# A layernorm, state-space convolution and gated unit on one core: the first spectra loads on GpSimd's queue, kept sums loaded behind SyncE's own stores, strict turns one chunk earlier, a pause cut in two

## The chip, the cores and the metric

The kernel runs on one core of a Trainium2 chip. The metric is the device time of one execution in microseconds (us); three runs of the kernel before gave a median of 709.12 us (707.67 to 710.72). One more execution was taken by the hardware profiler: 711.45 us, of which 709.7 us lie between the first and the last instruction (the span). All rows shown below come from that execution.

## What is computed

x is 2048 tokens by 448 channels. It is normalised per token, and the result goes through two independent branches whose sums are added to x. Branch A is a convolution with a kernel K of 2048 taps per channel, made from 256 complex exponentials per channel; the reference does it by Fourier transforms. Branch B is a gated unit with 1792 hidden features.

```python
P = jnp.exp((A * dt[:, None])[:, :, None] * pos[None, None, :])
K = 2.0 * jnp.einsum("dn,dnl->dl", C, P).real
y = irfft(rfft(u_t, 2 * L) * rfft(K, 2 * L))[:, :, :L]        # + u * D_skip
...
h = _sigmoid(xn @ w_gate) * (xn @ w_up)                       # 448 -> 1792
return x + _A_ref(xn, ...) + h @ w_down                       # 1792 -> 448
```

## The kernel before

Two generators record the work: `conv()` (branch A) and `glu()` (branch B). The loop at the end of the kernel decides which of them records its next piece: the one whose share `done[i] / total[i]` of its own planned cost is smaller. Each `yield` gives the planned cost of the piece just recorded (`WK` for a third of a chunk, `WS` for a spectra step, and so on). When the list `turns` is not empty, the loop alternates strictly between the two instead. A scheduler then arranges the recorded instructions of each engine at build time; `tc.issue_after(x)` asks that what follows stands behind `x`.

**Stages.** Until about 110 us the input is normalised and the tables for K are made. From 150 to 525 us, K is made in 56 chunks (`NCK`) of 8 channels, in `kgen`: TensorE spreads phases into PSUM (`tr`, L533), ScalarE takes sines of them (`S`, L541 to L544), VectorE multiplies them by magnitudes into `Et` and `Ft` (L602 to L604; there is one `Ft` buffer), and 64 small matmuls (`ko`, L618) contract them. Every fourth chunk is followed by `dm` (L628), a copy `ks` (L631) and 32 small matmuls, the first Fourier stage (`kp`, `kq`, L559), whose result goes to the DRAM buffer `sk_d`. GLU work stands between these: the gate and up projections (`gu`, L710, three matmuls for each product, since each operand is held as a high and a low part), then ScalarE's `th`, VectorE's `gu` product (L721), ScalarE's `hh` (L726), VectorE's `hl` (L728), and the down projections (`po`, L816, "downs" below), which VectorE adds to `acc` (L821). Half 0 of the tokens is done before half 1; between them, at about 265 to 350 us, the tokens of half 1 are normalised, turned and put through their own first stage (L207 to L290, L694). This is called the crossing below.

From 525 us on `spectra` runs 17 steps. A step loads `sx`, `skl` and for a new row `tb` (function `loads`, L864), does the forward stage `there` (64 matmuls `pk`, `px`, L901, from PSUM to `kk` and `xx` by VectorE, L907 and L908), the product (two VectorE multiplications L914 and L915, two GpSimd sums L917 and L918), `halves` (L922, L923), and one step later the inverse `back` (L936), whose result `vt` goes through DRAM (`v_d`). The pieces of `glu()` that are left stand between the steps. Steps are numbered from 0; three steps' loads (`NLD`) are recorded ahead. `bk` is the constant table of `back` and lies in the memory that `wk`, the table of the first Fourier stage, held; `wf` is the table of the last stage. `ac` (L1025) are sums of half 0 that were parked in DRAM and are loaded again; the program records these loads in steps 7 to 10, and the profile has them issued at 538.85 us (three) and 541.94 us, in the first steps. From 680 us the last inverse results go through DRAM once more and the output is stored.

The matmuls of one step are bound to the last GLU matmul recorded before them (`sp_mm`, `glu_mm`), so TensorE's order in the spectra is the order in which the two generators take turns.

Of the kernel before, what the change touches and what calls it, by code (L numbers as in the profile page):

```python
# [28 lines left out]
NFT = F // 128  # L29
WK = 4.3  # L30
WS = 5
HOLE = 6
AHEAD = 34
WP = 5
WX = 2
HELD = 9
LASTS = 2
HP = 300
Y0 = (8, 1)
CP = D // 4  # L40
H = D // 2
# [8 lines left out]
NLD = 3  # L50
NTB = 4
NCK = D // DC
# [74 lines left out]
def s4d_glu_kernel(ctx, tc, io):  # L127
    nc = tc.nc
# [11 lines left out]
    x1_d = dram.tile([2, 2, 32, 64, H], F32, name="x1_d")  # L140
    sk_d = dram.tile([2, 8, 128, 7, 128], F32, name="sk_d")
# [311 lines left out]
    def kgen(pk):  # L453
# [128 lines left out]
        for g in range(NCK // NCH):  # L582
            for c in range(NCH):
                cn = g * NCH + c
                S = nxt
                me, mf = (m[:, 2 * DC * (c % 2) : 2 * DC * (c % 2) + 2 * DC] for m in mags)
                of = (cn + 9) // NCH
                if NCH * of < NCK and cn and c != 6:
                    if c == 7 or cn == 1:
                        more = powers(pms, of, fts, sins[0])  # L590
                    next(more)
                    if cn < 3:
                        next(more)
                if cn + 1 < NCK:
                    nxt = ahead(cn + 1)
                    if c % 2 == 1:
                        squares(coming[0])
                yield WK / 3
                Et = tl[f"Et{cn % 2}"]
                Ft = tl["Ft"]  # L600
                two = lambda ap: ap.unsqueeze(1).to_broadcast([128, 2, 2 * DC, 32])
                v.tensor_tensor(Et[:, :, :, 32:64], two(me[:, :, 32:64]), S[:, 1::-1], ALU.mult)  # L602
                v.tensor_tensor(Et[:, :, :, 0:32], two(me[:, :, 0:32]), S[:, 1:3, :, ::-1], ALU.mult)  # L603
                fts[:] = [v.tensor_tensor(Ft, two(mf), S[:, 3:5], ALU.mult)]  # L604
                if cn + 2 < NCK and c % 2 == 0:
                    coming = magnitudes(cn // 2 + 1)
                if c % 2 == 1:
                    mags = coming
                yield WK / 3
                if cn % 4 == 0:  # L610
                    ko = psc[-1].tile([128, 8, 64], F32, name="ko", bufs=1)
                with tc.issue_after(glu_mm[0].ins):
                    for q in range(2):
                        sl = 2 * (cn % 4) + q
                        for k in range(4):
                            h, cc = k // 2, k % 2
                            for j in range(4):
                                nc.tensor.matmul(  # L618
                                    ko[32 * j : 32 * j + 32, sl],
                                    Ft[:, cc, DC * h + 4 * q + j],  # L620
                                    Et[:, cc, DC * h + 4 * q + j],
                                    start=(k == 0),
                                    stop=(k == 3),
                                    skip_group_check=True,
                                )
                if cn % 4 == 3:
                    ks = tl["ks"]
                    nc.tensor.matmul(  # L628
                        ko[:, :, 0], ident, dm[:, cn // 4], start=False, stop=True, skip_group_check=True
                    )  # L630
                    nc.scalar.copy(ks.rearrange("p s (q b) -> p s q b", q=2), ko.rearrange("p s (b q) -> p s q b", q=2))  # L631
                yield WK / 3
                if cn % 4 == 2 and cn > 3 or cn + 1 == NCK:

                    with hp(HP) if cn + 1 == NCK else tc.issue_after(glu_mm[0].ins):
                        first_stage((cn - 3) // 4 if cn + 1 < NCK else cn // 4)
# [94 lines left out]
    def glu():  # L731
        stores, later = [], []
        for half in range(2):
# [3 lines left out]
            for fs_ in ORDER[half]:  # L737
# [14 lines left out]
                for n_, (f, t) in enumerate(order):  # L752
# [39 lines left out]
                        wts.append((dh, dl))  # L792
                    if half == 1 and fs_ is ORDER[1][0] and n_ in (1, 3):
                        q = 2 + n_ // 2
                        with tc.issue_after(marks[1].ins):
                            x_load(accs[q], 4 * q, 4, [nc.scalar])
                    yield 2.5
                    for s_ in end[n_] if cross else ():
# [41 lines left out]
    def spectra(pf):  # L840
# [19 lines left out]
        def work(n, sh, bufs):  # L860
            return spare[n].pop() if spare.get(n) else pf.tile(sh, F32, name=n, bufs=bufs)

        def loads(h, k):
            sx = pf.tile([128, 4, H], F32, name="sx", bufs=NLD)  # L864
            sk = pf.tile([128, 7, 4, 32], F32, name="skl", bufs=NLD)
            if k == 32:
                to = sx[:, 0:2]
                nc.sync.dma_start(to, x1_d[:, :, :, ::32].rearrange("h q b c d -> (q b c) h d"))
                for i in range(2):
                    nc.sync.dma_start(sk[:, :, i], sk_d[i, 0, :, :, :32])  # L870
                return None, sk, sx
            rows = x1_d[h].rearrange("q b (c k) d -> (q b c) (k d)", c=2)
            nc.sync.dma_start(sx.rearrange("p k d -> p (k d)"), rows[:, H * k : H * k + 4 * H])
            if k not in tabs:
                tabs[k] = pf.tile([128, 4, 64], F32, name="tb", bufs=NTB)
                nc.sync.dma_start(tabs[k], io["c_tab"][k // 4])
            tb = tabs.pop(k) if h else tabs[k]

            nc.sync.dma_start(sk.rearrange("p g k d -> p g (k d)"), sk_d[h, k // 4])
            return tb, sk, sx  # L880

        def after():
            return tc.issue_after(sp_mm[0].ins)
# [42 lines left out]
        def back(h, k, sd, engs=(nc.sync, nc.sync)):  # L926
            vts.append(vts.pop(0))
            vt = vts[-1]
            n = 2 if k == 32 else 4
            bt = t32[:, 1:].rearrange("p (q e) m -> p q e m", q=2) if k == 32 else bk  # L930
            with after():
                for e in range(2):
                    for g in range(n):
                        s = slice(32 * g, 32 * g + 32)
                        for p in range(2):
                            mm = nc.tensor.matmul(  # L936
                                pb[g // 2][64 * p : 64 * p + 64, g % 2, :H], bt[s, p, e], sd[s, p, e],
                                start=(e == 0), stop=(e == 1), skip_group_check=True,
                            )
            sp_mm[:] = [mm]  # L940
            for j in range(n // 2):
                nc.scalar.copy(vt[:, 2 * j : 2 * j + 2], pb[j][:, :, :H])  # L942

            for p in range(2):
                s = slice(64 * p, 64 * p + 64)
                real = slice(64 * p, 64 * p + 64, 2)
                to = lambda h_: v_d[h_, s].rearrange("(c g q) w d -> w c g q d", c=2, g=4)
                if k == 32:
                    for j in range(2):
                        engs[p].dma_start(to(j)[:, 1, 0, 0], vt[real, j])  # L950
                elif k == 0:
                    engs[p].dma_start(to(h)[:, 0, 0, 0], vt[real, 0])
                    for c in range(2):
                        engs[p].dma_start(to(h)[:, c, 1:, 0], vt[64 * p + c : 64 * p + 64 : 2, 1:])
                else:
                    engs[p].dma_start(to(h)[:, :, :, k // 4], vt[s])  # L956

        def turned(h, k, n=8, eng=nc.sync):
            if h not in vp:
# [33 lines left out]
        steps = [(0, k) for k in ks] + [(1, k) for k in ks[-NTB:] + ks[:-NTB]]  # L993
        steps[3:3] = [(None, 32)]
        tabs = {}
        ld = [loads(*s) for s in steps[:NLD]]
        nc.gpsimd.dma_start(wf, io["c_wf"])
        prev, made, wait, due = None, None, [], []
        turns[:] = [0]
        for n, (h, k) in enumerate(steps):  # L1000

            end = n + 1 == len(steps)
# [11 lines left out]
                ld.append(loads(*steps[n + NLD]))  # L1014
            glu_on[:] = [1]
            yield WS / 2
            sp_mm[:] = glu_mm
            if ready is not None:
                back(*ready)
                if ready[1] < 32:  # L1020
                    wait.append(ready[:2])
            if 7 <= n < 11:
                o = slice(2 * n - 14, 2 * n - 12)
                with after():
                    nc.sync.dma_start(ac[:, o], acc_d[:, o])  # L1025

            while len(wait) > 2 and not (due and wait[0][0] == 1):
# [25 lines left out]
    def conv():  # L1053
        with tc.tile_pool(name="psk", bufs=1, space=PSUM) as ps_, tc.tile_pool(
# [78 lines left out]
                            yield from x_spec([xns[n - 2][:, b + i] for i in range(2)], 4 * (n - 2) + b)  # L1133
            with tc.tile_pool(name="pk", bufs=1, side="right", reuse_waits="tile") as pk:
                yield from kgen(pk)
        yield HOLE
        psc.append(ctx.enter_context(tc.tile_pool(name="psf", bufs=1, space=PSUM)))

        pa = ctx.enter_context(tc.tile_pool(name="pa", bufs=1, side="left", reuse_waits="tile"))
# [2 lines left out]
            yield from spectra(pf)  # L1142

    lasts, glu_mm, sp_mm, glu_on, x1s, hfs, xls = [], [], [], [], [0], [], []
    turns = []
    xq, psc, raws, acl, marks, slots, pqs = list(x_first), [], [], [], [None, None], {}, []
    W1s, GGs, act = [], [], []
    gens = [conv(), glu()]
    total = [sum(Y0) + 11 * WP + 8 * WX + AHEAD + NCK * WK + HOLE + 19 * WS, 2 * (4 + NFT * 14.8) - HELD]
    done = [0.0, 0.0]  # L1150
    done[0] += next(gens[0])
    held = False
# [41 lines left out]
```

## Time and profile before

| | |
|---|---|
| median of 3 runs | 709.12 us (707.67 to 710.72) |
| profiled execution | 711.45 us, span 709.7 us |
| TensorE busy | 658.4 us, 93% of the span, 8581 matmuls |
| VectorE, ScalarE, GpSimd busy | 577.1, 418.6 and 381.1 us (81%, 59%, 54%) |
| mean granted TensorE clock | 0.969 |
| DMA | 125.76 MB, mean 177 GB/s |

A row of a timeline gives the start in us, the duration in us, the engine (PE is TensorE, DVE is VectorE, ACT is ScalarE, POOL is GpSimd, SP is SyncE; a "q" behind the name marks the issuing of a DMA), the line of the kernel, the instruction with the tile that it writes and those that it reads, the count, and in brackets how long the engine was idle before it and what ended that. A row of the windows gives the stretch in us, its length, the busy time and count of each engine, the granted TensorE clock as a fraction, the busy share of the DMA engines and their GB/s.

### The profile page before, as it was taken

How to read it: one execution, taken by the hardware profiler on the slowest of the kernel's cores; microseconds unless marked ns; L12 is line 12 of the kernel's file. 1: busy time of each engine (PE TensorE's matmuls, PEld its weight loads, DVE VectorE, ACT ScalarE, POOL GpSimd, SP SyncE). 2: the span in 40 equal slices, each digit the busy share in tenths (PEclk: the TensorE clock that was granted, in tenths of full speed). 3: DMA queues.
4: the chain of work that ended last, by engine and by line, in shares of the span. 5: the costliest groups of instructions: out<-in, count | busy, mean ns of one | idle time of the engine just before them, and what ended most of it. 6: DMA issues, size and time to landing. Idle time of an engine off the chain costs nothing. (4 is left out here: it accounts for less than half of the span.)

```text
span 709.7 us, 20759 instructions
## 1 busy us (share of the span) xinstructions
PE 658.4 (93%) x8581; PEld 506.8 (71%) x8581; DVE 577.1 (81%) x779; ACT 418.6 (59%) x651; POOL 381.1 (54%) x395
## 2 busy tenths in 40 slices
PE   2998999999998899898899999999996999999994
PEld 1765778888876687564678788788884777777783
DVE  5789899589989898986568798799868888986753
ACT  3635636479888958787457877987842333332220
POOL 2111016586799999965246769889913344342101
PEclk9998999999999999797899999999999999999998
DMA  9987658655225633465575314333369878887366
GB/s 197 254 272 217 189 180 247 225 194 197 44 90 154 198 92 90 107 166 135 161 214 165 101 54 140 108 100 94 95 196 292 294 286 278 291 279 223 131 180 159
DMA packets 96638, 125.76 MB, mean 177 GB/s; under 512 B 12976, under 2 KB 82928, under 8 KB 96288
## 3 DMA queue, kind: packets, MB, share of 16 engines
q1 hardware_dynamic: 78688, 111.52, 51.0%
q10 hardware_dynamic: 17136, 11.01, 6.6%
q0 software_dynamic: 720, 1.90, 1.2%
q8 instruction: 68, 1.11, 0.7%
q14 instruction: 26, 0.21, 0.1%
HBM read 72.09 MB, written 52.30 MB: 175 GB/s over the span
## 5 line engine op out<-in xcount | busy, mean ns | idle before, releaser
L511 POOL TENSOR_TENSOR me<-me,pm 128x32 f32<-128x32 f32 (+1 forms) x168 | 157.2, 935 | 71.8 <-DVE Et L603 58.8
L511 POOL TENSOR_TENSOR mf<-mf,pm 128x64 f32<-128x64 f32 (+1 forms) x112 | 115.8, 1034 | 6.5
L710 PE MATMUL gu<-xh,wh 128*128 128x512 f32 x336 | 101.9, 411 | 2.4 <-DVE hl L728 1.0
L710 PE MATMUL gu<-xl,wh 128*128 128x512 f32 x336 | 96.7, 393 | 0.0
L710 PE MATMUL gu<-xh,wl 128*128 128x512 f32 x336 | 96.3, 392 | 0.0
L816 PE MATMUL po<-dh,hh 128*128 128x448 f32 (+1 forms) x227 | 88.5, 390 | 3.6 <-ACT x L694 1.8
L602 DVE TENSOR_TENSOR Et<-me,S 128x1024 f32<-128x1024 f32 x56 | 75.9, 1357 | 14.6 <-ACT S L544 8.2
L816 PE MATMUL po<-dh,hl 128*128 128x448 f32 (+1 forms) x227 | 86.0, 379 | 0.7 <-DVE hl L728 0.7
L603 DVE TENSOR_TENSOR Et<-me,S 128x1024 f32<-128x1024 f32 x56 | 77.4, 1382 | 10.9 <-ACT me L524 10.0
L816 PE MATMUL po<-dl,hh 128*128 128x448 f32 (+1 forms) x227 | 85.7, 377 | 0.0
L604 DVE TENSOR_TENSOR Ft<-mf,S 128x1024 f32<-128x1024 f32 x56 | 80.8, 1442 | 5.8 <-ACT S L544 3.3
L917 POOL TENSOR_TENSOR yy<-yy 128x448 f32<-128x448 f32 (+1 forms) x16 | 31.0, 1940 | 91.1 <-DVE yy L914 91.1
L710 PEld LDWEIGHTS gu<-xh,wh 128*128 128x128 f32 x336 | 60.8, 191 | 25.6 <-issue 9.0
L726 ACT CAST hh<-gu 128x512 fp32r<-128x512 f32 x56 | 33.2, 594 | 72.1 <-DVE gu L721 65.0
L541 ACT ACTIVATE S<-tr 128x1024 f32<-128x1024 f32 x56 | 58.2, 1039 | 25.8 <-PE tr L533 14.2
L710 PEld LDWEIGHTS gu<-xh,wl 128*128 128x128 f32 x336 | 62.9, 188 | 14.5 <-DVE fr L305 0.7
L618 PEld LDWEIGHTS ko<-Et,Ft 128*32 128x32 f32 x3584 | 55.3, 113 | 24.7 <-issue 9.8
L710 PEld LDWEIGHTS gu<-xl,wh 128*128 128x128 f32 x336 | 62.7, 188 | 14.1 <-issue 0.7
L618 PE MATMUL ko<-Et,Ft 128*32 128x64 f32 x3584 | 65.4, 225 | 6.0 <-DVE Ft L604 5.6
L821 DVE SCALAR_TENSOR_TENSOR acc<-po,acc 128x448 f32<-128x448 f32 (+1 forms) x81 | 48.8, 610 | 24.8 <-PE po L816 24.8
L544 ACT ACTIVATE S<-S,hpi 128x1024 f32<-128x1024 f32 x56 | 66.2, 1181 | 0.0
L542 ACT ACTIVATE S<-tr 128x1024 f32<-128x1024 f32 x56 | 58.1, 1037 | 0.0
(204 smaller groups left out, 1263.0 us busy)
## 6 DMA issues: line engine op xcount, KB each, us to landing
wt_d<-wh SPq DMA_DIRECT2D x14, 512.0 KB
wt_d<-wl SPq DMA_DIRECT2D x14, 512.0 KB
sk_d<-sk ACTq DMA_DIRECT2D x28, 256.0 KB
wl<-wt_d SPq DMA_DIRECT2D x14, 512.0 KB
wh<-wt_d SPq DMA_DIRECT2D x14, 512.0 KB
sx<-x_d SPq DMA_DIRECT2D x16, 448.0 KB
skl<-sk_d SPq DMA_DIRECT2D x16, 448.0 KB
vp<-v_d SPq DMA_DIRECT2D x7, 896.0 KB
```

The costliest lines, as they stand in the source:

```text
L511: ins = nc.gpsimd.tensor_tensor(m[:, :, w + a : 2 * w : n], m[:, :, a:w:n], par(base + i).unsqueeze(2).to_broadcast([128, 4 * DC, w // n]) ...
L541: nc.scalar.activation(rows(cs), pv, AF.Abs)
L542: nc.scalar.activation(rows(S[:, 0:5:4]), pv, AF.Sin, scale=TWO_PI)
L544: sins[:] = [nc.scalar.activation(cs, cs, AF.Sin, scale=-TWO_PI, bias=hpi)]
L602: v.tensor_tensor(Et[:, :, :, 32:64], two(me[:, :, 32:64]), S[:, 1::-1], ALU.mult)
L603: v.tensor_tensor(Et[:, :, :, 0:32], two(me[:, :, 0:32]), S[:, 1:3, :, ::-1], ALU.mult)
L604: fts[:] = [v.tensor_tensor(Ft, two(mf), S[:, 3:5], ALU.mult)]
L618: nc.tensor.matmul(ko[32 * j : 32 * j + 32, sl], Ft[:, cc, DC * h + 4 * q + j], Et[:, cc, DC * h + 4 * q + j], start=(k == 0), stop=(k == ...
L710: glu_mm[:] = [nc.tensor.matmul(ps, a_, b_, start=(n == 0), stop=(n == len(mm) - 1))]
L726: nc.scalar.copy(hh, hf)
L816: glu_mm[:] = [nc.tensor.matmul(po[:, ds], a_[:, bs], w_[:, ds], start=(n == 0), stop=(n == 3 * fc - 1))]
L821: v.scalar_tensor_tensor(acc[:, b, ds], po[:, ds], 0.5, acc[:, b, ds], ALU.mult, ALU.add)
```

## The change

Six edits. (1) The pause `HOLE` between `kgen` and `spectra`, one piece of cost 6, becomes two pieces of 2.5; `total` follows, so all shares shift slightly. (2) `turns` is set when the last chunk begins its third piece and not at the start of the spectra. (3) The eight loads of x into the sums of half 1 (`x_load`, issued by ScalarE) are bound to ScalarE's own `th` (`marks[0]`) in place of VectorE's product (`marks[1]`). (4) The nine loads of steps 0 to 2 are issued by GpSimd and not by SyncE. (5) The four `ac` loads are bound to the last `v_d` store of SyncE and not to a matmul. (6) `sp_mm` is reset only where a `back` follows.

```diff
-HOLE = 6
+HOLE = 2
...
+                if cn + 1 == NCK:
+                    turns[:] = [1]
                 yield WK / 3
...
-                        with tc.issue_after(marks[1].ins):
+                        with tc.issue_after(marks[0].ins):
                             x_load(accs[q], 4 * q, 4, [nc.scalar])
...
-        def loads(h, k):
+        def loads(h, k, eng=nc.sync):
...
-            nc.sync.dma_start(sx.rearrange("p k d -> p (k d)"), rows[:, H * k : H * k + 4 * H])
+            eng.dma_start(sx.rearrange("p k d -> p (k d)"), rows[:, H * k : H * k + 4 * H])
...
-                    engs[p].dma_start(to(h)[:, :, :, k // 4], vt[s])
+                    stored[:] = [engs[p].dma_start(to(h)[:, :, :, k // 4], vt[s])]
...
-        ld = [loads(*s) for s in steps[:NLD]]
+        ld = [loads(*s, nc.gpsimd) for s in steps[:NLD]]
         nc.gpsimd.dma_start(wf, io["c_wf"])
...
-        turns[:] = [0]
+        stored.clear()
...
-            sp_mm[:] = glu_mm
             if ready is not None:
+                sp_mm[:] = glu_mm
                 back(*ready)
...
-                with after():
+                with tc.issue_after(stored[0].ins):
                     nc.sync.dma_start(ac[:, o], acc_d[:, o])
...
-        yield HOLE
+        for _ in range(HOLE):
+            yield 2.5
...
-    total = [... + NCK * WK + HOLE + 19 * WS, ...]
+    total = [... + NCK * WK + HOLE * 2.5 + 19 * WS, ...]
```

Three places where the order of an engine's instructions moves. The first is the end of `kgen` on TensorE. The `ko` rows are the last two chunks, 54 and 55, the others matmuls of the last two gates. Of before:

```order
L710 MATMUL gu<-xh,wh 128x512 x3
L710 MATMUL gu<-xr,wh 128x512
L710 MATMUL gu<-xh,wl 128x512 x3
L710 MATMUL gu<-xr,wl 128x512
L618 MATMUL ko<-Et_1182,Ft 32x64 x32
L710 MATMUL gu<-xl,wh 128x512 x3
L710 MATMUL gu<-xh,wh 128x512 x3
L710 MATMUL gu<-xr,wh 128x512
L710 MATMUL gu<-xh,wl 128x512 x3
L710 MATMUL gu<-xr,wl 128x512
L710 MATMUL gu<-xl,wh 128x512 x3
L618 MATMUL ko<-Et_1177,Ft 32x64 x32
```

And of the change, the last gate, the same two chunks, and `dm` behind them:

```order
L712 MATMUL gu<-xl,wh 128x512 x3
L712 MATMUL gu<-xh,wh 128x512 x3
L712 MATMUL gu<-xr,wh 128x512
L712 MATMUL gu<-xh,wl 128x512 x3
L712 MATMUL gu<-xr,wl 128x512
L712 MATMUL gu<-xl,wh 128x512 x3
L618 MATMUL ko<-Et_1182,Ft 32x64 x32
L618 MATMUL ko<-Et_1177,Ft 32x64 x32
L628 MATMUL ko<-dm,ident 128x8
```

Between the two chunks stood 14 gate matmuls; now nothing does. On VectorE at the same place the last chunk's products (`Et_1177` and `Ft`) stood ahead of the last gate's `gu` and `hl`, and four `acc` rows followed before the first spectra step. Of before:

```order
L602 TENSOR_TENSOR Et_1177<-me_1180,S_1179 128x32x32
L603 TENSOR_TENSOR Et_1177<-me_1180,S_1179 128x32x32
L604 TENSOR_TENSOR Ft<-mf_1181,S_1179 128x1024
L721 SCALAR_TENSOR_TENSOR gu<-th,gu 128x512
L728 TENSOR_TENSOR hl<-gu,hh 128x512
L821 SCALAR_TENSOR_TENSOR acc<-po,acc 128x448 x4
L907 TENSOR_TENSOR kk<-pk,oo 128x448
```

And of the change:

```order
L603 TENSOR_TENSOR Et_1177<-me_1180,S_1179 128x32x32
L723 SCALAR_TENSOR_TENSOR gu<-th,gu 128x512
L730 TENSOR_TENSOR hl<-gu,hh 128x512
L604 TENSOR_TENSOR Ft<-mf_1181,S_1179 128x1024
L823 SCALAR_TENSOR_TENSOR acc<-po,acc 128x448 x2
L909 TENSOR_TENSOR kk<-pk,oo 128x448
L910 TENSOR_TENSOR kk<-pk,oo 128x448
L909 TENSOR_TENSOR xx<-px,oo 128x448
L910 TENSOR_TENSOR xx<-px,oo 128x448
L916 TENSOR_TENSOR yy<-kk,xx 128x896
L823 SCALAR_TENSOR_TENSOR acc<-po,acc 128x448
L917 TENSOR_TENSOR xx<-kk,xx 128x896
```

`Ft` of the last chunk moved behind `gu` and `hl`, and two of the four `acc` additions moved from before step 0 to behind it. The second place is GpSimd's queue at the end of `kgen`. Of before, the last magnitude row, the two constant tables and the product sums of the spectra:

```order
L511 TENSOR_TENSOR mf_1181<-mf_1181,pm_1186 128x32x16
L997 DMA wf<-in_c_wf_dram 128x1024
L991 DMA bk<-in_c_bk_dram 128x256
L917 TENSOR_TENSOR yy<-yy 128x2x224
L918 TENSOR_TENSOR yy<-xx 128x2x224
```

And of the change:

```order
L999 DMA wf<-in_c_wf_dram 128x1024
L993 DMA bk<-in_c_bk_dram 128x256
L875 DMA sx<-x_d 128x896
L878 DMA tb<-in_c_tab_dram 128x256
L881 DMA skl<-sk_d 128x896
L875 DMA sx<-x_d 128x896
L878 DMA tb<-in_c_tab_dram 128x256
L881 DMA skl<-sk_d 128x896
L875 DMA sx<-x_d 128x896
L878 DMA tb<-in_c_tab_dram 128x256
L881 DMA skl<-sk_d 128x896
L919 TENSOR_TENSOR yy<-yy 128x2x224
```

The nine loads moved from SyncE to GpSimd, and all of them stand behind `bk`. The third place is the crossing on TensorE, chunks 25 and 26 (the `ko` rows), with the phases `tr` of the chunks that follow. Of before:

```order
L618 MATMUL ko<-Et_1177,Ft 32x64 x5
L207 MATMUL gu<-ident,xt 128x128 x4
L618 MATMUL ko<-Et_1177,Ft 32x64 x3
L207 MATMUL gu<-ident,xt 128x128 x2
L618 MATMUL ko<-Et_1177,Ft 32x64 x24
L533 MATMUL tr<-sel,ph_1188 128x512 x2
```

And of the change:

```order
L533 MATMUL tr<-sel,ph_1188 128x512 x2
L207 MATMUL gu<-ident,xt 128x128 x4
L618 MATMUL ko<-Et_1177,Ft 32x64 x5
L207 MATMUL gu<-ident,xt 128x128 x2
L618 MATMUL ko<-Et_1177,Ft 32x64 x27
```

The `tr` pair moved from behind the chunk to in front of it. In both, six downs and the next `tr` pair (`ph_1187`) follow.

More of the change, by code (lines that the diff above doesn't have):

```diff
@@ L867, in loads @@
                 to = sx[:, 0:2]
-                nc.sync.dma_start(to, x1_d[:, :, :, ::32].rearrange("h q b c d -> (q b c) h d"))
+                eng.dma_start(to, x1_d[:, :, :, ::32].rearrange("h q b c d -> (q b c) h d"))
                 for i in range(2):
-                    nc.sync.dma_start(sk[:, :, i], sk_d[i, 0, :, :, :32])
+                    eng.dma_start(sk[:, :, i], sk_d[i, 0, :, :, :32])
                 return None, sk, sx
             rows = x1_d[h].rearrange("q b (c k) d -> (q b c) (k d)", c=2)
-            nc.sync.dma_start(sx.rearrange("p k d -> p (k d)"), rows[:, H * k : H * k + 4 * H])
+            eng.dma_start(sx.rearrange("p k d -> p (k d)"), rows[:, H * k : H * k + 4 * H])
             if k not in tabs:
                 tabs[k] = pf.tile([128, 4, 64], F32, name="tb", bufs=NTB)
-                nc.sync.dma_start(tabs[k], io["c_tab"][k // 4])
+                eng.dma_start(tabs[k], io["c_tab"][k // 4])
             tb = tabs.pop(k) if h else tabs[k]
-            nc.sync.dma_start(sk.rearrange("p g k d -> p g (k d)"), sk_d[h, k // 4])
+            eng.dma_start(sk.rearrange("p g k d -> p g (k d)"), sk_d[h, k // 4])
             return tb, sk, sx
@@ L1144, in s4d_glu_kernel @@
     lasts, glu_mm, sp_mm, glu_on, x1s, hfs, xls = [], [], [], [], [0], [], []
-    turns = []
+    turns, stored = [], []
     xq, psc, raws, acl, marks, slots, pqs = list(x_first), [], [], [], [None, None], {}, []
@@ L1148, in s4d_glu_kernel @@
     gens = [conv(), glu()]
-    total = [sum(Y0) + 11 * WP + 8 * WX + AHEAD + NCK * WK + HOLE + 19 * WS, 2 * (4 + NFT * 14.8) - HELD]
+    total = [sum(Y0) + 11 * WP + 8 * WX + AHEAD + NCK * WK + HOLE * 2.5 + 19 * WS, 2 * (4 + NFT * 14.8) - HELD]
     done = [0.0, 0.0]
```

## The prediction

> **What bounds the kernel now.** I read the windows first, from the end of the kernel generation on.
>
> ```profile
> 533.00:555.00 22.00, 16.63 (x282) 11.74 (x283) 18.79 (x28) 5.04 (x10) 8.57 (x6) 0.92 0.95 302
> 555.00:600.00 45.00, 45.00 (x620) 32.10 (x619) 37.44 (x57) 16.71 (x33) 15.67 (x10) 1.00 0.83 290
> 600.00:650.00 50.00, 50.00 (x744) 36.94 (x742) 40.78 (x64) 14.19 (x28) 18.85 (x12) 1.00 0.86 276
> ```
>
> From 555 to 650 TensorE is busy all the time at full clock, and the order behind the fourth step is the same in both programs: there nothing is to be won or lost unless a load comes late. So the end moves by what happens before 555. Between 533 and 555 TensorE is idle for 22 - 16.63 = 5.4 us while DMA is 0.95 busy; that is where edits 2, 4 and 5 work. Next the two largest waits of TensorE behind the chunks' start, over the whole span (us in total, times, longest):
>
> ```profile
> PE tr L533 <- ACT S L543: 6.3, 5, 2.6
> PE ko L618 <- DVE Ft L604: 5.6, 4, 2.9
> ```
>
> Both lie within the chunks, where the shifted interleaving of edit 1 decides. Now the transition on TensorE and, below it, on VectorE:
>
> ```profile
> 523.61 0.84 PE L710 MATMUL gu<-xl,wh 128*128 128x512 f32 x3
> 524.38 1.10 PE L618 MATMUL ko<-Et,Ft 128*32 128x64 f32 x64
> 527.57 0.47 PE L816 MATMUL po<-dh,hh 128*128 128x448 f32 x1
> 532.33 0.37 PE L816 MATMUL po<-dh,hl 128*128 128x448 f32 x1
> 533.26 0.99 PE L901 MATMUL pk<-skl,tb 64*32 64x224 f32 x32 [0.56 <-DMA skl<-sk_d]
> 536.54 0.99 PE L901 MATMUL pk<-skl,tb 64*32 64x224 f32 x32 [1.54 <-DMA skl<-sk_d]
> 543.48 0.99 PE L901 MATMUL pk<-skl,tb 64*32 64x224 f32 x32 [2.19 <-DVE acc L821]
> 547.92 0.99 PE L936 MATMUL pk<-xx,bk 32*64 32x224 f32 x16 [1.27 <-issue]
> ```
>
> ```profile
> 521.81 1.21 DVE L604 TENSOR_TENSOR Ft<-mf,S 128x1024 f32<-128x1024 f32 x1
> 524.56 0.70 DVE L721 SCALAR_TENSOR_TENSOR gu<-th,gu 128x512 f32<-128x512 f32 x1 [1.54 <-PE gu L710]
> 525.91 0.69 DVE L728 TENSOR_TENSOR hl<-gu,hh 128x512 fp32r<-128x512 f32 x1 [0.65 <-ACT hh L726]
> ...
> 534.91 0.62 DVE L907 TENSOR_TENSOR kk<-pk,oo 128x448 f32<-128x448 f32 x1 [1.55 <-ACT oo L905]
> ...
> 544.25 0.62 DVE L821 SCALAR_TENSOR_TENSOR acc<-po,acc 128x448 f32<-128x448 f32 x1
> 544.78 1.78 DVE L915 TENSOR_TENSOR xx<-kk,xx 128x896 f32<-128x896 f32 x1
> ...
> 547.21 0.61 DVE L908 TENSOR_TENSOR kk<-pk,oo 128x448 f32<-128x448 f32 x1
> ```
>
> The reader sees three things. The last chunk's `Ft` was made 2.6 us before its matmuls, behind a gate that stood between the last two chunks. Steps 0 and 1 wait for `skl`. And from 534.91 VectorE runs without a gap until the first `back` at 547.92, which starts as soon as `kk` of step 2 (547.21 + 0.61) has freed its PSUM: from step 0's start S = 533.26 on, VectorE is the bound, and `back` comes at S + 14.66, whatever the loads of steps 1 and 2 do.
>
> **The chunk end (edits 1 and 2): +2.45.** The two `ko` groups now stand next to each other, and `Ft`, of which there is one buffer, stands behind `gu` and `hl`. Let the last gate end at T. In the old rows T is 524.38, where TensorE took up `ko` behind that gate, and VectorE's `gu` starts at T + 0.18 and ends at T + 0.88; `hh` by ScalarE and `hl` follow, and `hl` ends at T + 2.2 (525.91 + 0.69 - 524.38); `Ft` takes 1.21, so T + 3.4, and the last chunk starts at about T + 3.5. TensorE is ready for it when chunk 54 is through, at T + 1.05. The wait is **2.45 us**, and nothing hides it: TensorE's next rows need this chunk. Bounds: 2.2 to 2.8; it can't be below 1.2, since `Ft` can't start before chunk 54 has read the buffer.
>
> **The loads of steps 0 to 2 (edit 4): +1.4.** The old and new issuers:
>
> ```profile
> 525.87 0.38 SPq L879 DMA_DIRECT2D skl<-sk_d  x1
> ...
> 538.85 1.31 SPq L1025 DMA_DIRECT2D ac<-acc_d  x3
> ```
>
> ```profile
> 528.00 0.54 POOL L991 DMA_DIRECT2D bk<-in_c_bk_dram  x1 [11.27 <-PE kq L559]
> ```
>
> SyncE issued step 0's `skl` 1.7 us before the first-stage matmuls ended (E = 527.57, where the downs begin), its `sx` and `tb` before it. On GpSimd they stand behind `bk`, which waits for the last `kq` and was issued at E + 0.43. At 0.54 for an issue, `sx` follows at E + 1.0, `tb` at 1.5, `skl` at 2.1. When does that land? The old `skl` took from 525.87 to 533.26, 7.4 us, with DMA full; the quiet `wf` load of 512 KB took 3.7 us to landing, `bk` in the busy stretch 6.8:
>
> ```profile
> wf<-in_c_wf_dram POOLq DMA_DIRECT2D x1, 512.0 KB, 3.7
> ```
>
> So `skl` lands between E + 5.8 and E + 9.5. Counting bytes, `bk`, `sx`, `tb`, `skl` (128 + 448 + 128 + 448 KB) and the 0.5 MB that ScalarE stores to `sk_d` at the same time are about 1.7 MB, 5 to 6 us at the 302 GB/s of the window: E + 7.1 is my value. Step 0 started at E + 5.69 before; it starts **1.4 us later**, bounds +0.1 and +3.8. Its twelve downs less in front don't hide this: by the rows of 527.57 and 532.33, 24 downs begin within 4.8 us, so 12 are through at E + 2.5, and TensorE is idle for some 4.6 us. What steps 1 and 2 no longer wait (1.54 and 2.19) isn't gained, since VectorE is the bound there. GpSimd's first product sums stand behind the last `skl` on that queue; they are due at S + 4, and the last issue waits for step 0's `sx` to land, about S: covered.
>
> The Trainium skill, page "DMA: Bandwidth & Descriptors", section "Rules for kernel authors", says that spreading DMAs over SyncE, ScalarE and GpSimd gives no bandwidth and saves only issue time. The DMA share of 0.95 in the row of 533 to 555 bears this out, and by it this term would be the later issue alone, without any gain from a second queue, which is how it is summed.
>
> **Two additions change sides (edit 2): +1.07.** Two of the four `acc` rows that VectorE did while TensorE ran downs before step 0 now stand between step 0 and the first `back`, on the stretch where VectorE has no gap. The row at 544.25 starts 0.53 before its successor: 2 x 0.53 = 1.07 us, `back` at S + 15.7. Lower bound 0, if `L915` runs its usual 1.09 and not 1.78; upper 1.3.
>
> **Transition: 2.45 + 1.4 + 1.07 = +4.9**, bounds +2.3 and +7.9. Since the work between E and the first `back` is the same, this shift reaches the end undiminished.
>
> **The `ac` loads (edit 5): 0.** Three left SyncE's queue at 538.85, 1.8 MB in all; now they stand in steps 7 to 10, at about 590 to 625, where DMA is 0.83 to 0.86 busy and TensorE full. They leave room in a stretch that VectorE bounds, and enter one whose loads are three steps ahead; bounds -0.5 and +1. Edit 6 moves no row: 0.
>
> **The crossing (edits 1 and 3): -3.** The shares shift by under 1%, but that is enough to reorder TensorE between chunks 17 and 28. The stalls there, and what they did to the clock:
>
> ```profile
> 218.00 1.10 PE L618 MATMUL ko<-Et,Ft 128*32 128x64 f32 x64 [1.89 <-DVE Ft L604]
> 291.48 1.50 PE L618 MATMUL ko<-Et,Ft 128*32 128x64 f32 x46 [2.86 <-DVE Ft L604]
> 325.36 0.74 PE L533 MATMUL tr<-sel,ph 128*128 128x512 f32 x2 [2.02 <-ACT S L543]
> 327.09 1.96 PE L272 MATMUL gu<-xt,wx 32*64 32x448 f32 x8 [0.99 <-DVE xl L214]
> ```
>
> ```profile
> 290.00:295.00 5.00, 3.52 (x68) 2.56 (x68) 4.96 (x6) 2.94 (x7) 4.84 (x8) 0.56 0.62 177
> ...
> 325.00:330.00 5.00, 3.65 (x14) 1.16 (x16) 5.00 (x8) 5.00 (x8) 1.28 (x1) 0.81 0.29 92
> 330.00:335.00 5.00, 5.00 (x13) 1.64 (x10) 1.18 (x2) 2.45 (x7) 3.31 (x6) 0.50 0.32 73
> 335.00:340.00 5.00, 5.00 (x78) 3.91 (x77) 1.46 (x3) 1.12 (x3) 0.00 (x0) 0.66 0.62 142
> ```
>
> The stall at 291.48 stays: VectorE's rows there are the same. At 325.36 the `tr` pair waits for the sines of the pair before it, which now stands in front of chunk 25 and not behind it. The stall of 2.02 should shrink to about 0.9, the next of 0.99 stays or grows to 1.4. The clock then ran at 0.81, 0.50 and 0.66: busy time times what was missing is 3.65 x 0.19 + 5 x 0.50 + 5 x 0.34 = 4.9 us. Whether that goes is open: two gaps of 0.9 and 1.4 close together may or may not halve the clock. So -0.7 without it, -6 with it; I take -3, the middle, since no row decides. Against it, four loads of x stand in a row on ScalarE ahead of a group of sines; in this trace two of them held it for 2.65 us:
>
> ```profile
> 353.17 2.65 ACTq L236 DMA_DIRECT2D acc<-in_A_u_dram  x2
> ```
>
> That is 0 to +2 where TensorE has nothing else, and 0 here, as TensorE went on working then.
>
> **Sum:** +4.9 - 3 = +1.9. On the profiled execution's 711.45 this gives 713.35; that execution was 2.3 us above the median, so I state it against the median: 709.12 + 1.9 = **711.0**.
>
> **The rivals.** *Faster:* the crossing's halved clock vanishes (-6, or -7 with the whole stall), and the transition comes out near its low bounds (+2.45, +0.1, 0). -7 + 2.55 = -4.4, so 704.7. For it: the `tr` pair is a full chunk earlier. Against it: the DMA share of 0.95, and `bk` ahead of the loads.
>
> *Slower:* TensorE's idle time before step 0 halves its clock. The place is E + 2.5 to E + 7.1. A gap of 1.89 us at 218.00 was followed by full clock, one of 2.86 at 291.48 by 0.56; the case decides when the gap exceeds something between these, and I expect 4.6. Its price is that of the dip that the old transition had after its own gaps,
>
> ```profile
> 548.00:551.00 3.00, 2.88 (x35) 2.06 (x36) 3.00 (x6) 1.06 (x2) 0.00 (x0) 0.83 0.99 316
> 551.00:554.00 3.00, 3.00 (x29) 1.77 (x31) 2.16 (x3) 0.01 (x1) 2.29 (x2) 0.60 0.98 333
> ```
>
> 2.88 x 0.17 + 3 x 0.40 = 1.7 us, beside +4.9 and with only -0.7 of the crossing: +5.9, so 715.0. The Trainium skill, page "TensorE: Matmul & The Clock Gate", section "What's actually happening", puts the fall to half clock at one idle window of about 3.4 us; by it my gap of 4.6 us is over the mark, the one of 2.86 was not, though the clock of 0.56 says that it fell. The trace decides for the lower mark.
>
> *No effect:* the moved loads don't change what bounds, and gains and losses cancel within 1 us: 709 to 710, inside the forecast's own range.
>
> **How the numbers follow.** About 0.5% (3.5 us) is what a measurement of this kernel can tell from no change. Forecast, with the no-effect case: 0.42, 711.0, own range 706 to 712.6. Faster: 0.25. Slower: 0.33, since its first terms are read from an order that is fixed and only the crossing can pay for them. The range of 8 in 10 reaches from 704 to 717.5: below to the faster rival's price, above to the slower rival's with the late bound of the loads.
>
> **What would show it.** A new wait of `ko` on `Ft` of 2.2 to 2.8 us at the last chunk; step 0's `pk` waiting 4 to 5 us for `skl`, and none of the two old waits at steps 1 and 2; the first `back` some 15.7 us behind step 0; the granted clock around 325 to 340 near 1 or near 0.5, and after step 0 below 1. The prediction is wrong if `skl` lands at E + 4 or earlier, if TensorE isn't full from 560 on, or if another stretch of the chunks, which I read as unchanged, stalls.

## The result, and the profile after

The changed kernel took 718.17 us (median of 6 runs, 713.45 to 720.15), the kernel before 710.34 us beside it (6 runs, 707.67 to 712.58). The ratio is 1.0092 with a 95% interval of 1.0064 to 1.0121: slower by 0.9%, 4.5 to 8.6 us. The profiled execution has a span of 718.4 us and a mean granted clock of 0.959, against 709.7 us and 0.969.

The windows of the changed kernel, in the stretches shown of before (length, busy time and count of PE, PEld, DVE, ACT and POOL, granted clock, DMA share, GB/s):

```profile
533.00:555.00 22.00, 15.03 (x230) 10.68 (x228) 13.75 (x21) 3.20 (x6) 7.65 (x11) 0.84 0.91 289
555.00:600.00 45.00, 43.74 (x550) 30.17 (x558) 36.27 (x56) 14.27 (x28) 17.63 (x12) 0.92 0.68 219
600.00:650.00 50.00, 50.00 (x770) 36.71 (x755) 42.94 (x66) 16.42 (x32) 22.02 (x14) 1.00 0.91 310
```

The stretch in which TensorE is full now begins later, behind the first `back`, and is as full as it was. The transition on TensorE:

```profile
522.09 1.10 PE L618 MATMUL ko<-Et,Ft 128*32 128x64 f32 x64
525.92 1.74 PE L618 MATMUL ko<-Et,Ft 128*32 128x64 f32 x64 [2.74 <-DVE Ft L604]
527.59 0.60 PE L628 MATMUL ko<-dm,ident 128*128 128x8 f32 x2
...
530.78 0.74 PE L818 MATMUL po<-dh,hh 128*128 128x448 f32 x1
...
539.58 1.75 PE L903 MATMUL pk<-skl,tb 64*32 64x224 f32 x32 [5.08 <-DMA skl<-sk_d]
...
556.26 1.18 PE L938 MATMUL pk<-xx,bk 32*64 32x224 f32 x16 [3.15 <-DVE kk L910]
```

The last chunk waits 2.74 us for `Ft`, and step 0 waits 5.08 us for `skl`. The chunk itself then takes 1.74 us in place of 1.10, and step 0's `pk` 1.75 in place of 0.99: TensorE ran at half speed after both gaps, as the clock in shorter windows of the same stretch shows (the clock is the third figure from the end of a row).

```profile
525.00:527.00 2.00, 1.07 (x49) 1.08 (x53) 0.87 (x1) 0.00 (x0) 0.00 (x0) 0.80 1.07 379
527.00:530.00 3.00, 2.33 (x71) 2.06 (x64) 0.00 (x0) 0.59 (x1) 0.00 (x0) 0.50 0.38 118
530.00:533.00 3.00, 3.00 (x38) 2.67 (x34) 0.00 (x0) 1.12 (x2) 1.10 (x3) 0.50 0.11 40
533.00:536.00 3.00, 1.50 (x8) 1.05 (x6) 1.25 (x2) 0.00 (x0) 3.00 (x6) 1.00 0.85 185
536.00:539.00 3.00, 0.00 (x0) 0.00 (x0) 0.00 (x0) 0.00 (x0) 1.22 (x3) 0.57 1.05 397
539.00:542.00 3.00, 2.42 (x56) 1.73 (x64) 0.01 (x1) 0.53 (x1) 0.00 (x0) 0.50 1.01 402
```

GpSimd's queue in that stretch:

```profile
531.21 0.54 POOL L993 DMA_DIRECT2D bk<-in_c_bk_dram  x1 [14.95 <-PE kq L559]
532.45 0.54 POOL L875 DMA_DIRECT2D sx<-x_d  x1 [0.70 <-ACT sk L565]
532.97 0.54 POOL L878 DMA_DIRECT2D tb<-in_c_tab_dram  x1
533.51 0.54 POOL L881 DMA_DIRECT2D skl<-sk_d  x1
```

Nothing goes out between 516 and 531 us while GpSimd waits to issue `bk`; step 0's `skl` leaves 2.7 us after the first downs began (E = 530.78) and lands 6 us later.

Measured from landmark to landmark, the 8.3 us by which the first `back` is later (556.26 against 547.92) come about so:

| stretch | before, us | after, us | difference |
|---|---|---|---|
| start to the end of the gates (chunk 54 taken out) | 523.3 | 522.1 | -1.2 |
| end of the gates to chunk 55 (chunk 54 in it) | 1.05 | 3.83 | +2.8 |
| chunk 55 to E, the first down | 3.19 | 4.86 | +1.7 |
| E to S, step 0 | 5.69 | 8.80 | +3.1 |
| S to the first `back` | 14.66 | 16.68 | +2.0 |
| the first `back` to the end of the span | 161.78 | 162.14 | +0.4 |

One execution of each stands behind these differences, and that of the change, 720.15 us, is the slowest of its six; the medians of the two kernels are 7.8 us apart.

### The profile page after: what moved, and what is told of

Read it like the earlier page. It is cut to its first block, busy times and chain, and to the rows that moved or that the text cites. A ratio compares the mean times of both kernels' runs of the same rounds, so it can differ in the third digit from the quotient of the medians.

```text
span 718.4 us, 20772 instructions
## 1 busy us (share of the span) xinstructions
PE 662.4 (92%) x8581; PEld 510.6 (71%) x8581; DVE 578.1 (80%) x779; ACT 418.2 (58%) x651; POOL 376.5 (52%) x404
## 5 line engine op out<-in xcount | busy, mean ns | idle before, releaser
L511 POOL TENSOR_TENSOR me<-me,pm 128x32 f32<-128x32 f32 (+1 forms) x168 | 146.5, 872 | 74.5 <-DVE Et L603 61.7
L511 POOL TENSOR_TENSOR mf<-mf,pm 128x64 f32<-128x64 f32 (+1 forms) x112 | 120.2, 1073 | 6.4
L604 DVE TENSOR_TENSOR Ft<-mf,S 128x1024 f32<-128x1024 f32 x56 | 79.1, 1413 | 9.7 <-PE ko L618 5.9
```

The source lines that it names most:

```text
L511: ins = nc.gpsimd.tensor_tensor(m[:, :, w + a : 2 * w : n], m[:, :, a:w:n], par(base + i).unsqueeze(2).to_broadcast([128, 4 * DC, w // n]) ...
```

## The experiments

All were timed against the kernel before. "The change" is the changed kernel, E the first down behind the first-stage matmuls, S the start of step 0. The table has the ratio to before with its interval, and the stretch from E to the first `back` in the profiled execution of each, which is 20.35 us in before and 25.48 us in the change.

| run | ratio (95%) | median, us | E to S, us | E to `back`, us |
|---|---|---|---|---|
| the change | 1.0092 (1.0064 to 1.0121) | 718.17 | 8.80 | 25.48 |
| bk last | 1.0059 (1.0023 to 1.0096) | 713.9 | 3.68 | 20.88 |
| loads on SyncE | 0.9995 (0.9961 to 1.0028) | 708.85 | 3.79 | 19.24 |
| turns late | 1.0095 (1.0064 to 1.0127) | 715.34 | 8.84 | 25.25 |
| pause only | 1.0032 (0.9996 to 1.0067) | 710.96 | 7.04 | 20.91 |
| bk fourth | 1.0007 (0.9972 to 1.0042) | 710.44 | 3.39 | 18.84 |
| chunks apart, loads on SyncE | 0.9962 (0.9927 to 0.9997) | 705.43 | 3.50 | 18.42 |
| old pause, loads on SyncE | 1.0068 (1.0037 to 1.0098) | 713.59 | 6.19 | 22.89 |
| small edits | 1.0044 (1.0013 to 1.0075) | 710.63 | 6.72 | 22.86 |
| both mended, loads on GpSimd | 0.9970 (0.9940 to 1.0000) | 708.7 | 3.20 | 19.03 |
| no reset (edit 6 alone) | 1.0034 (1.0013 to 1.0055) | 711.52 | 5.23 | 20.63 |
| GpSimd only (edit 4 alone) | 1.0066 (1.0042 to 1.0090) | 714.36 | 8.85 | 24.76 |
| chunks apart, loads late | 1.0067 (1.0044 to 1.0091) | 714.8 | 8.77 | 25.29 |

### Where the late loads come from

**bk last.** The only difference from the change is that `bk` is issued behind the nine loads.

```diff
-        nc.gpsimd.dma_start(bk, io["c_bk"])
...
         nc.gpsimd.dma_start(wf, io["c_wf"])
+        with tc.issue_after(tail[0].ins):      # tail: the last skl load
+            nc.gpsimd.dma_start(bk, io["c_bk"])
```

> The changed kernel with one DMA moved: bk is issued behind the nine loads on GpSimd's queue, not ahead of them; every other row of every engine stands as in the change. Theory 1 (the loads are late because bk ahead of them waits for the last first-stage matmul): sx of step 0 goes out about 8 us earlier, right after the last chunk's Et; step 0 starts when its 12 downs are through, some 3.7 us after E in place of 8.8, so about 5 us are won of the change's 8. Theory 2 (GpSimd's queue itself is slow, wherever bk stands): step 0 still waits over 3 us for skl, and less than 2 us are won. Theory 3 (VectorE bounds the stretch to the first back anyway): step 0 starts earlier, but back moves by under 2 us.

**Loads on SyncE.** Edit 4 undone.

```diff
-        ld = [loads(*s, nc.gpsimd) for s in steps[:NLD]]
+        ld = [loads(*s) for s in steps[:NLD]]
```

> The changed kernel with edit 4 undone: the nine loads on SyncE again; TensorE's and VectorE's order as in the change. Theory 1: the same gain as with bk last, about 5 us, within 1 us of that run. Theory 2: it gains about 5 us where the run with bk last gains under 2. Theory 3: under 2 us, like the other.

Step 0 started 3.68 and 3.79 us after E, so in both its loads were there when the twelve downs were through: `bk` was what held them. But with the loads on SyncE the whole loss of the change is gone (0.9995), while with `bk` last 0.6% stay. Neither theory had this. The trace of the run with `bk` last, on ScalarE behind the last first-stage matmuls:

```profile
532.37 0.61 ACT L565 COPY sk<-kp 128x512 f32<-128x512 f32 x1 [4.99 <-DMA sk_d<-sk]
532.87 0.65 ACT L565 COPY sk<-kq 128x512 f32<-128x512 f32 x1
533.55 2.27 ACTq L567 DMA_DIRECT2D sk_d<-sk  x2
535.86 0.53 ACT L907 COPY oo<-pk 128x448 f32<-128x448 f32 x1 [2.34 <-PE px L903]
```

and its GpSimd queue, the first and the last of the nine loads:

```profile
515.20 0.54 POOL L875 DMA_DIRECT2D sx<-x_d  x1 [0.58 <-ACT me L524]
...
520.23 0.54 POOL L881 DMA_DIRECT2D skl<-sk_d  x1 [0.61 <-DMA sx<-x_d]
```

The nine loads, 3 x (448 + 128 + 448) KB = 3.1 MB, went out within 5.6 us. ScalarE had issued its store of `sk` at 519.71 into that burst; `sk` has one buffer, so the copy for the last first stage waited 4.99 us until the store was through. In the run with the loads on SyncE the same copy waited 2.09 us for the matmuls alone and began 0.1 us after E; here it began 3.0 us after E, so the store held it for about 2.9 us. The next stores and `oo` of step 0 stand behind it on ScalarE: `oo` begins 2.8 us after S where it took 1.1 with the loads on SyncE (534.16 against S = 533.07), and the first `back` comes 1.6 us later after E.

**bk fourth.** Step 0's three loads ahead of `bk`, the other six behind it; else the change. This is the test of the burst.

```diff
-        ld = [loads(*s, nc.gpsimd) for s in steps[:NLD]]
+        ld = [loads(*steps[0], nc.gpsimd)]
         nc.gpsimd.dma_start(wf, io["c_wf"])
+        with tc.issue_after(tail[0].ins):
+            bks = [nc.gpsimd.dma_start(bk, io["c_bk"])]
+        with tc.issue_after(bks[0].ins):
+            ld += [loads(*s, nc.gpsimd) for s in steps[1:NLD]]
```

> The changed kernel with bk behind step 0's three loads and ahead of the other six on GpSimd's queue; all other rows as in the change. With bk behind all nine, step 0 started 3.7 us after E, but ScalarE's copy into sk waited 5.0 us for its store, and VectorE's first kk came 1.7 us later than with the loads on SyncE. Theory 1 (3 MB issued at once crowd out the store; the queue itself is as good as SyncE's): with 1 MB ahead of bk the copy no longer waits, the first back comes 19.3 us after E, and the time is within 1.5 us of the run with the loads on SyncE, 5.5 to 7 us under the change. Rival (any use of GpSimd's queue at this place costs): it stays 3 us or more above the run with the loads on SyncE.

```profile
529.38 0.62 ACT L565 COPY sk<-kp 128x512 f32<-128x512 f32 x1 [2.09 <-PE kq L559]
529.88 0.62 ACT L565 COPY sk<-kq 128x512 f32<-128x512 f32 x1
```

ScalarE's copy now waits for the matmul and not for the store, the first `back` comes 18.84 us after E, and the time is 1.0007 of before. So GpSimd's queue as such costs nothing that can be measured here; its order does, 0.85% between the change and this run, with TensorE's order the same. The intervals of this run and of the one with `bk` last overlap (0.9972 to 1.0042 against 1.0023 to 1.0096), so the price of the burst rests on the two traces, 2.0 us from E to `back`, more than on the medians.

**GpSimd only.** The kernel before with edit 4 alone.

```diff
-        ld = [loads(*s) for s in steps[:NLD]]
+        ld = [loads(*s, nc.gpsimd) for s in steps[:NLD]]
```

> The kernel before with edit 4 alone: TensorE's order is that of before, 24 downs ahead of step 0, the nine loads behind bk on GpSimd's queue. Theory 1: step 0 starts 8.8 us after E and not 5.7, and the clock may halve in the gap: +3 to +5 us on before. Rival (the late loads matter only where few downs stand in front): under +1.5 us.

1.0066, which is +4.7 us: as theory 1 had it. E to S is 8.85 us although 24 downs stand in front of step 0, and E to `back` is 24.76 us, 4.4 longer than in before.

### The last chunk

**Turns late.** Edit 2 undone.

```diff
-                if cn + 1 == NCK:
-                    turns[:] = [1]
...
+        turns[:] = [0]
```

> The changed kernel with edit 2 undone: strict turns only from the spectra on, so 18 and 6 downs stand ahead of steps 0 and 1 and not 12 and 12; chunks 54 and 55 still stand side by side. Theory 1: step 0 starts when skl lands, as in the change; one VectorE addition leaves the stretch to the first back: -0.5 us, not to be told from nothing; the wait of the last chunk for Ft stays at 2.7 us. Rival (the strict turns themselves cost, and put the two chunks together): the wait is gone and 3 us or more are won.

**Pause only.** The kernel before with edit 1.

```diff
-HOLE = 6
+HOLE = 2
...
-        yield HOLE
+        for _ in range(HOLE):
+            yield 2.5
```

> The kernel before with edit 1 alone: the pause as two pieces of 2.5, with total to match. Theory 1: the order of the chunks becomes that of the change; the last chunk waits 2.7 us for Ft, the halved clock after it costs 1.7 us more, the chunks ahead give back 1.2: about +3 us on before. Rival (the crossing's gain outweighs it, the loss of the change being all in the loads): -3 to 0 us.

The last chunk's row on TensorE in the run with turns late:

```profile
521.75 1.10 PE L618 MATMUL ko<-Et,Ft 128*32 128x64 f32 x64 [2.74 <-DVE Ft L604]
```

In the run with the pause only:

```profile
528.02 1.10 PE L618 MATMUL ko<-Et,Ft 128*32 128x64 f32 x64 [2.74 <-DVE Ft L604]
```

And in the run with chunks apart and loads on SyncE (below):

```profile
520.46 1.08 PE L618 MATMUL ko<-Et,Ft 128*32 128x64 f32 x58 [0.29 <-issue]
```

With edit 1 and without edit 2 the wait is there, to the hundredth; so the shorter pause puts the chunks together and not the strict turns. Turning edit 2 off changed nothing that can be measured (1.0095 against 1.0092). Edit 1 alone is +2.3 us, with an interval that just holds 0: expected +3.

**Chunks apart.** Loads on SyncE, and strict turns from the third chunk from the end on.

```diff
-                if cn + 1 == NCK:
+                if cn + 3 == NCK:
                     turns[:] = [1]
```

> The run with the loads on SyncE (edit 4 undone), and strict turns from the third chunk from the end on: ten downs stand between chunks 54 and 55. Theory 1 (chunk 55 pays for standing next to chunk 54: 2.7 us of wait and about 1.5 us of halved clock after it): the wait for Ft is gone and 3 to 4 us are won on the run with the loads on SyncE, about 705 us. Rival (the wait is only passed on, to the end of the gates or to step 0): within 1.5 us of that run.

**Chunks apart, loads late.** The same edit on the change itself.

> The change with strict turns from the third chunk from the end on, so ten downs stand between chunks 54 and 55; loads on GpSimd behind bk as in the change. Theory 1: the loads are timed from the last first-stage matmul, so the wait at chunk 55 and the late loads add up: 3 to 4 us under the change, still 2 to 3 us above before. Rival (one hides in the other): under 1.5 us won.

**Both mended.** The same edit with `bk` fourth, so the loads stay on GpSimd.

> The change with both losses mended and the loads kept on GpSimd: strict turns from the third chunk from the end on (ten downs between chunks 54 and 55) and bk behind step 0's three loads. Theory 1 (the late loads and the chunks side by side are the change's loss, the queue isn't): within 1.5 us of the run with chunks apart and loads on SyncE, about 705 us, 0.4 to 0.8% under before. Rival (GpSimd's early loads crowd the weight loads of the last gates): 2 us or more above that run.

The wait at the last chunk is gone in all three. Against their partners without the edit the ratios fall from 0.9995 to 0.9962, from 1.0092 to 1.0067 and from 1.0007 to 0.9970: 0.33, 0.25 and 0.37%, or 1.8 to 2.6 us, against 3 to 4 expected. In each pair the intervals overlap; that all three fall by about the same, whether the loads are late or not, speaks for two losses that add up, with neither hidden in the other. The second is smaller than the wait and its halved clock in the trace, and the stretch from E to `back` hardly moved. The traces show a new loss at the end, in all three runs and in none of their partners. With more downs done among the chunks, no gate matmuls are left between the last spectra steps, and TensorE waits there; in the run with the loads on SyncE:

```profile
665.83 0.99 PE L938 MATMUL pk<-xx,bk 32*64 32x224 f32 x16 [1.27 <-DVE kk L910]
672.06 1.08 PE L938 MATMUL pk<-xx,bk 32*64 32x224 f32 x5 [2.56 <-DVE xx L924]
```

In the 40 us that end 10 us before the span's end, TensorE is idle for 5.1, 3.2 and 4.9 us in the three runs (in the order named above) and for 1.0, 1.2 and 1.0 us in the partners, and its clock there is 0.91, 0.87 and 0.96 against 1.00. No run tried another place for these downs. The run with chunks apart and loads on SyncE is the fastest of all: 0.9962, with an interval that ends just below 1. That is a gain of about 2.7 us, below the half per cent that I would claim from a single comparison, though the run with both mended points the same way.

### The other edits

**Old pause, loads on SyncE.** Edits 1 and 4 undone, edit 2 kept.

> The change with edits 1 and 4 undone: the chunks in the order of before, strict turns from the last chunk on, so 6, 12 and 12 downs ahead of steps 0 to 2, loads on SyncE. Theory 1: no wait for Ft at chunk 55, but step 0 is bound by its loads as before (5.7 us after E), with only 6 downs to cover it: 0 to +1 us on before. Rival (strict turns are what gains): 2 us or more under before.

**Small edits.** Edits 3, 5 and 6 on the kernel before.

> The kernel before with edits 3, 5 and 6 alone (loads of x behind th, ac behind v_d stores, no reset of sp_mm). Theory 1: the four ac loads leave 539 to 545 us and enter a stretch that TensorE fills: 0, within 1 us of before. Rival (the 1.8 MB of ac held back the loads of the first steps): 2 us or more under before.

**No reset.** Edit 6 alone on the kernel before.

```diff
-            sp_mm[:] = glu_mm
             if ready is not None:
+                sp_mm[:] = glu_mm
                 back(*ready)
```

> The kernel before with edit 6 alone: sp_mm is reset only where a back follows, which moves 6 of the 24 downs from ahead of step 0 to between steps 0 and 1; nothing else moves on TensorE. Theory (edit 6 is what the run of the small edits lost): the first back comes about 22.9 us after E and not 20.4, +2 to +3 us on before. Rival (ac or the loads of x cost it): within 1 us of before.

The run with the old pause was expected within 1 us of before and came out 4.8 us slower. It has edits 3, 5 and 6 too, which alone cost 3.1 us (next paragraph); the rest, 1.7 us, is what strict turns add to them, and their intervals overlap. On the old order of the chunks, strict turns leave 6 downs ahead of step 0, TensorE waits 4.71 us for `skl`, and the clock falls again:

```profile
532.53 1.86 PE L903 MATMUL pk<-skl,tb 64*32 64x224 f32 x32 [4.71 <-DMA skl<-sk_d]
```

The small edits cost 3.1 us (0.9 to 5.3) where 0 was expected, and edit 6 alone 2.4 us (0.9 to 3.9). Edit 6 does move TensorE: 18 and 6 downs stand ahead of steps 0 and 1 and not 24 and 0. But the reason given for its price does not hold: in the profiled execution of edit 6 alone the stretch from E to `back` is 20.63 us, not 22.9, and its span of 708.7 us is shorter than that of before. What it costs on the median is not seen in the one trace there is, and stays open; so does whether `ac` or the loads of x cost anything beside it, which was not tried alone.

## Why the prediction was right or wrong

**What bounds the kernel: right.** TensorE is full behind the transition in both, and from the first `back` to the end the two differ by 0.4 us. The whole change of the time was in front of it.

**The chunk end, +2.45: right.** It was 2.74 us in all six traces in which edit 1 leaves the two chunks side by side. Its cause was put down to edits 1 and 2 together; the runs put it on edit 1 alone. What the term left out is the clock behind the gap. It was at 0.50 from 527 to 533 us, and chunk 55 to E took 1.7 us longer (0.8 to 1.9 us in the six traces).

**The loads, +1.4: right in mechanism, too small by half.** E to S grew by 3.1 us, inside the bounds of +0.1 to +3.8. The term that was mis-sized is the landing at E + 7.1: it was E + 8.8. Some 0.6 us of that is a later issue (`skl` at E + 2.7 in place of 2.1, since GpSimd paused for 0.70 us between `bk` and `sx`), and 1.1 us a landing that took 6.1 us against the 5.0 in my sum. The 1.5 and 2.2 us of waits that steps 1 and 2 had in before are gone, and as forecast nothing was gained by it.

**Two additions, +1.07: right, and again the clock on top.** S to `back` grew by 2.0 us; `kk` of step 0 came 2.4 us after S and not 1.65, since `pk` and `px` ran at half speed. That leaves 1.3 us for the additions.

**The `ac` loads, 0: not contradicted; edit 6, "moves no row": wrong.** Under the change's strict turns it is not seen, but alone on before it moves six downs and costs 2.4 us.

**The crossing, -3: right on the wait for the sines, wrong on the rest and as a sum.** The wait for the sines is gone, and new ones came at the same place. The stall of 2.86 us at 291.48, which was to stay, is gone too: 0.94 us at 286.94, with a new one of 2.28 us behind it. On TensorE, after:

```profile
286.94 1.10 PE L618 MATMUL ko<-Et,Ft 128*32 128x64 f32 x64 [0.94 <-DVE Ft L604]
293.11 0.97 PE L272 MATMUL gu<-xt,wx 32*64 32x448 f32 x4 [2.28 <-DVE xr L220]
322.08 2.19 PE L272 MATMUL gu<-xt,wx 32*64 32x448 f32 x12 [2.11 <-DVE hl L730]
...
436.74 1.10 PE L618 MATMUL ko<-Et,Ft 128*32 128x64 f32 x64 [1.74 <-DVE Ft L604]
490.91 0.27 PE L559 MATMUL kq<-wk,ks 64*64 64x64 f32 x1 [1.74 <-issue]
```

```profile
295.00:300.00 5.00, 5.00 (x74) 3.15 (x74) 3.68 (x3) 4.91 (x9) 5.00 (x6) 0.50 0.87 200
...
325.00:330.00 5.00, 5.00 (x31) 2.73 (x30) 2.11 (x4) 2.25 (x6) 3.32 (x6) 0.50 0.63 143
330.00:335.00 5.00, 5.00 (x105) 3.83 (x105) 3.17 (x6) 1.78 (x3) 0.80 (x2) 0.84 0.32 75
```

The clock still fell to 0.50 at both places, though for a shorter time. The last two waits of the first fence lie in chunks 39 to 51, which I had read as unchanged, and where before had none over 0.4 us: they take 3.5 us back, and the second cost clock as well (below). The step that failed is the reading that no other stretch of the chunks would stall; the prediction named it as what would make it wrong. The net of edit 1 up to the last gate is -1.2 us in this pair of traces, and the run with edit 1 alone says that the whole of it does not gain. One pair can't size this term: the gates (chunk 54 taken out, as in the table) end between 517.9 and 524.2 us in the six traces with the chunks side by side, and between 518.9 and 523.3 in the five with the old pause.

**The case that happened** is the rival named slower: a halved clock around the transition, and a crossing that pays little, 715.0. The ratio times the 709.12 us shown with the prediction gives 715.6. The place was only half right: the clock fell before step 0, as foreseen, and already at the last chunk, after a gap of 2.74 us. That 715.0 lies so near is partly luck. Its sum was +5.9 and the ratio gives +6.5, but in the pair of traces the first `back` comes 8.3 us later: the loads cost 1.7 us more than in that sum and the halved clock 0.7 us more (2.4 against 1.7). The likeliest case, 711.0, was wrong because its one gain, the crossing, was taken at the middle of its bounds, the loads were too small by 1.7 us, and the clock behind the two gaps, which the same trace priced, was left to a rival.

**A length of gap that decides, between 1.89 and 2.86 us: wrong.** The prediction's own trace has a gap of 1.81 us at 348.93 with a clock of 0.65 and 0.50 in the two windows of 2 us from 348 on. After, the gap of 1.74 us at 490.91 was followed by half speed, the one of the same length at 436.74 by full clock:

```profile
492.00:494.00 2.00, 2.00 (x7) 1.52 (x6) 2.00 (x2) 1.34 (x3) 1.92 (x2) 0.52 0.03 8
494.00:496.00 2.00, 2.00 (x7) 1.59 (x6) 1.87 (x2) 0.59 (x1) 1.92 (x2) 0.63 0.00 0
```

And in the run with `bk` fourth a gap of 2.60 us left the clock at 1.00:

```profile
242.12 0.73 PE L533 MATMUL tr<-sel,ph 128*128 128x512 f32 x2 [2.60 <-ACT S L543]
242.00:244.00 2.00, 1.88 (x8) 1.42 (x8) 2.00 (x2) 2.00 (x5) 1.92 (x2) 1.00 0.90 349
244.00:246.00 2.00, 1.63 (x68) 1.44 (x68) 2.00 (x4) 2.00 (x4) 1.92 (x3) 1.00 0.52 201
```

The same wait of about 1.9 us for `Ft` near 217 us stands in all 14 traces: the clock stayed at 1.00 behind it in eight and fell to between 0.50 and 0.60 in six. The one of 2.6 us for the sines near 242 us stands in eight: the clock fell in five and stayed in three. Every gap of 2.74 us and more between 150 and 690 us in these traces was followed by a fall. What decides below that is not shown. The Trainium skill, page "TensorE: Matmul & The Clock Gate", section "What's actually happening", gives about 3.4 us of idle time for the fall; the six traces with a gap of 2.74 us show it below that.

## What to carry to other kernels

A DMA moved to another queue takes the place of its row there: look at what the rows ahead of it wait for, and at what else goes out if they don't. Moving `bk` behind the three urgent loads won back 0.85% here, moving it behind all nine only 0.33%. And price a wait with the clock that it halves: behind the gap of 2.74 us here that was another 0.8 to 1.9 us, which belongs into the sum and not into a rival.

## What the runs showed of the hardware that was not expected

Four things. The gap of 2.74 us at the last chunk was followed by a clock near 0.5 in each trace that has it: in the run with the pause alone 0.61 and 0.50 in the two windows of 2 us that follow, in the run with `bk` fourth 0.50 and 0.50. Shorter gaps, of 1.7 to 2.6 us, halved the clock in some executions and not in others, at the same row. Loads that nobody waits for yet can hold an unrelated engine: 3.1 MB put out within 5.6 us kept ScalarE's stores of 256 KB from landing for so long that its next copy began some 2.9 us late. And GpSimd stood idle for 0.70 us between two DMA issues (`bk` and `sx`), where those that follow start 0.53 us apart with no gap; the profile names ScalarE's copy for it, and the cause was not tried.
